# Packed attention and two MLPs on one core: the last 64 tokens of each sequence on all 128 partitions

## The chip, the cores and the metric

The kernel runs on one core of a Trainium2 chip. The metric is the device time of one launch in microseconds (us); the kernel before takes 1620.88 us in the median of three runs (1620.12 to 1622.61). The engines are PE (TensorE, matrix products; PEld is its loading of weights), DVE (VectorE), ACT (ScalarE), POOL (GpSimd) and SP (SyncE, which here only issues DMAs).

## What is computed

```python
def _attn_ref(q, k, v, p):              # q, k, v: 8 x 8 x 576 x 64; p: 8 x 8 x 32 x 64
    scale = 1.0 / np.sqrt(q.shape[-1])
    def sm_attn(qq, kk, vv):
        s = scale * np.matmul(qq, kk.transpose(0, 1, 3, 2))
        s = s - np.max(s, axis=-1, keepdims=True)
        a = np.exp(s)
        a = a / (np.sum(a, axis=-1, keepdims=True) + 1e-09)
        return np.matmul(a, vv)
    p_packed = sm_attn(p, k, v)
    return sm_attn(q, p_packed, p_packed)

x = attn_out.transpose(0, 2, 1, 3).reshape(4608, 512)
xn = x / rms(x) * rms_g                 # first MLP, d_ff 1536
x = (silu(xn @ w_gate) * (xn @ w_val)) @ w_out
h = x @ w_in2                           # second MLP, d_ff 2048
out = (h * sigmoid(1.702 * h)) @ w_out2
```

All inputs and the output are 32-bit floats.

## The kernel before

The 64 attention problems (8 batches of 8 heads) are worked in 16 chains: one chain is four heads of one batch. A chain loads its k, v and q (`load_kp`, `load_v`, `load_q`), transposes k and q on PE (`heads_t`, L297), multiplies p with k (`scores`, L308), takes the softmax (`s1`), transposes its weights (`a_t`, L341), multiplies them with v (`pv`, L353), transposes the result (`pp_t`, L374), multiplies it with q (`s2`), and forms the attention output (`x`, L443) for the row norm, whose reciprocal `ri` is spread over the partitions by five more transposes (`scale`, L474), once for each batch.

A sequence has 576 tokens: NC = 5 pieces, four of 128 and one of REST = 64. `GROUPS` puts pieces 0 and 1 into half e = 0 and pieces 2, 3 and 4 into half e = 1. The last piece lies in partitions 0 to 63 of its tile; `size(c)` is 64 for it and 128 otherwise, and cuts the partitions that an instruction reads. The letter a counts the two pairs of heads of a chain: a transpose takes two heads (2 x 64 columns) at a time. So a chain has ten transposes of k and ten of q, two of each on 64 rows.

The first four chains (LEAD, the lead below) run at the start in full 32-bit precision, with their own pool and loads of k in one piece (`kw`, then a copy on DVE into `kn`). The other twelve split each operand into a rounded high part and a low part (`split`: a copy on ACT, a subtraction on DVE or POOL; `split_v` for v), and three products stand for one. They are put between the matmuls of the first MLP (`mlp1`: `prods` L679, `gateval` L712, `project` L748), which is paced by a list of ns that each of its steps is taken to last. The second MLP (`mlp2`, L1068 and L1140) follows.

The order on each engine is set by a scheduler that works from the program order and its own estimate of times; only instructions marked `keep_in_program_order` stay where they are written, among them the loads of the chains after the lead. All loads are issued by SP, one after the other. Before each one but the first eight, SP waits for the landing of the load that stands eight before it. The tiles of the transposes, scores and products are PSUM banks: 3 of the 8 belong to attention (`ap`), 5 to the MLP (`mm`).

Of the kernel before, what the change touches and what calls it, by code (L numbers as in the profile page):

```python
# [32 lines left out]
def tile_pack_attention__then__two_mlps(  # L33
# [24 lines left out]
    P = 128  # L58
# [89 lines left out]
    def attention(at, first, lp, psum, getL, getAT):  # L148
# [37 lines left out]

        def load_kp(n):
# [5 lines left out]
            rest = k[b, h0 : h0 + HG, S - REST :].rearrange("h p d -> p h d")  # L193
            if n < WIDE:
                kw = at.tile([P, HG, NC - 1, D], F32, tag="kq", name="kw", bufs=nb)
                load(n, kw, k[b, h0 : h0 + HG, : S - REST].rearrange("h (p c) d -> p h c d", c=NC - 1))
                load(n, kn[:REST, NC - 1], rest)
                for a in range(2):
                    hs = slice(2 * a, 2 * a + 2)
                    nc.vector.tensor_copy(kn[:, : NC - 1, hs].rearrange("p c h d -> p h c d"), kw[:, hs])  # L200
            else:
                for h in range(HG):
                    load(n, 
                        kn[:, : NC - 1, h, :], k[b, h0 + h, : S - REST].rearrange("(p c) d -> p c d", c=NC - 1)
                    )
                load(n, kn[:REST, NC - 1], rest)
# [9 lines left out]
        def load_v(n):  # L216
# [6 lines left out]
            vs = vn[:, :head].rearrange("p (h c d) -> p h c d", h=HG, d=D), vn[:REST, head:]  # L223
# [7 lines left out]
        def load_q(n):  # L231
            b, g = chains[n]
            qn = at.tile([P, NC, HG, D], F32, tag="kq", name="qn", bufs=2)
            hs = slice(HG * g, HG * g + HG)
            rest = q[b, hs, S - REST :].rearrange("h p d -> p h d")
            for h in range(HG):
                load(n, 
                    qn[:, : NC - 1, h, :], q[b, HG * g + h, : S - REST].rearrange("(c p) d -> p c d", p=P)
                )
            load(n, qn[:REST, NC - 1], rest)  # L240
            st[n]["qn"] = qn

        def split_v(n):
# [6 lines left out]
            head = (NC - 1) * HG * D  # L250
            for part in ((slice(None), slice(head)), (slice(REST), slice(head, NC * HG * D))):
                i = nc.scalar.copy(vh[part], vn[part])
                if n == LEAD:
                    tc.keep_in_program_order(i)
                nc.gpsimd.tensor_sub(vl[part], vn[part], fl(vh[part]))
            st[n]["v"] = vh, vl

        def v_of(t, c):
# [4 lines left out]
            return t[:REST, head:].rearrange("p (h d) -> p h d", h=HG)  # L263
# [21 lines left out]
        def heads_t(n, name, a, e):  # L285
# [9 lines left out]
            for c in GROUPS[e]:  # L295
                o = c * P - cols.start
                nc.tensor.transpose(  # L297
                    ps[:, o : o + size(c)],
                    src[: size(c), c, 2 * a : 2 * a + 2, :].rearrange("p h d -> p (h d)"),
                    ident[: size(c), : size(c)],  # L300
                )
            split([t[:, a, cols] for t in st[n][name + "T"]], ps[:, : cols.stop - cols.start], nc.vector)
# [30 lines left out]
        def a_t(n, e):  # L333
# [6 lines left out]
            for i, c in enumerate(GROUPS[e]):  # L340
                nc.tensor.transpose(ps[: size(c), i], e1[:, c * P : c * P + size(c)], ident)  # L341
            c0, c1 = GROUPS[e][0], min(GROUPS[e][-1] + 1, NC - 1)
            split([t[:, c0:c1] for t in st[n]["aT"]], ps[:, : c1 - c0], nc.vector)
            if NC - 1 in GROUPS[e]:
                split([t[:REST, NC - 1] for t in st[n]["aT"]], ps[:REST, NC - 1 - c0], nc.vector)

        def pv(n):
# [115 lines left out]
        def scale(b, *es):  # L463
# [5 lines left out]
            for e in es:  # L469
                ps = psum()  # L470
                cols = span(e)
                for c in GROUPS[e]:
                    o = c * P - cols.start
                    nc.tensor.transpose(  # L474
                        ps[:, o : o + size(c)],
                        ri[: size(c), c : c + 1].to_broadcast([size(c), P]),
                        ident[: size(c), : size(c)],
# [896 lines left out]
```

## Time and profile before

| | before |
|---|---|
| median of three runs | 1620.88 us |
| the profiled execution's own time | 1620.02 us |
| its span in the trace | 1618.2 us |
| PE busy | 1593.0 us (98%) |
| DVE, ACT, POOL busy | 68%, 54%, 57% |
| chain that ended last | PE 90%; DMA, DVE, ACT, issue 2% each |
| granted PE clock | 0.998 |

The profile is of one execution; 1.8 us of that execution's own time lie outside of the span. Busy time of PE runs from a matmul's start to its modelled end, and matmuls overlap, so what one matmul costs is read from the distance of the starts of two that follow each other. `128*128 128x256` in a row of PE is the weights (rows*columns) and the moving operand.

### The profile page before, as it was taken

The numbers are of one execution on the slowest core, as the hardware profiler recorded it, in microseconds if no ns is written. First come the engines' busy times: TensorE is split into PE (matmuls) and PEld (weight loads), VectorE is DVE, ScalarE is ACT, GpSimd is POOL, SyncE is SP. The second block draws the span as 40 slices with busy tenths as digits, with TensorE's granted clock in tenths as the row PEclk, the third lists the DMA queues.
The fourth block names the chain that finished last, engine by engine and source line by source line (L and its number), as shares of the span: only waits on it lengthen the run. The fifth ranks groups of instructions, "written<-read, shape, count | busy, mean of one in ns | idle before, by whom it ended". The sixth has DMA issues, their size and how long they took to land.

```text
span 1618.2 us, 29102 instructions
## 1 busy us (share of the span) xinstructions
PE 1593.0 (98%) x10608; PEld 1510.4 (93%) x10608; DVE 1094.5 (68%) x1899; ACT 870.6 (54%) x1799; POOL 915.7 (57%) x749
## 2 busy tenths in 40 slices
PE   7999999999999999999999999999999999999998
PEld 5699999999999999999999899999999999999998
DVE  5777777767777766676775567754685467468466
ACT  5677777666566655665665353534344434435432
POOL 3547777656655566563655275664466445546442
PEclk9999999999999999999999999999999999999999
DMA  9766666775556665475454887786677667888874
GB/s 263 222 175 185 210 198 215 255 222 184 180 176 210 204 193 180 150 250 204 153 204 149 316 282 241 235 248 187 183 225 248 189 186 240 288 247 252 285 232 143
DMA packets 217725, 348.21 MB, mean 215 GB/s; under 512 B 93936, under 2 KB 123632, under 8 KB 211440
## 3 DMA queue, kind: packets, MB, share of 16 engines
q1 hardware_dynamic: 217584, 346.35, 66.9%
q8 instruction: 85, 1.39, 0.4%
q14 instruction: 56, 0.46, 0.1%
HBM read 279.19 MB, written 67.11 MB: 214 GB/s over the span
## 4 chain that ended last, share of the span: by engine, by line
PE 90%; DMA 2%; DVE 2%; ACT 2%; issue 2%; POOL 1%; SPq 0%; POOLq 0%; DVEq 0%; ACTq 0%
PE ps_dn L1140 21%; PE ps_up L1068 20%; PE ps_o L748 18%; PE ps_g L712 18%; PE ps_w L679 4%; PE ps_at L308 3%; PE ps_at L297 2%; PE ps_at L353 2%; PE ps_at L443 2%; DMA kw<-in_k_dram 1%; DMA vn<-in_v_dram 1%; POOL ol L1114 1%; PE ps_at L341 0%; DMA raw<-in_moe_w_out_dram 0%; DVE Wl L684 0%
## 5 line engine op out<-in xcount | busy, mean ns | idle before, releaser
L1114 POOL TENSOR_TENSOR ol<-g,oh 128x1024 fp32r<-128x1024 f32 (+1 forms) x117 | 258.9, 2223 | 295.7 <-ACT oh L1112 292.9
L1140 PE MATMUL ps_dn<-wo,oh 128*128 128x256 f32 x2016 | 366.2, 283 | 1.8 <-ACT oh L1112 0.9
L1140 PEld LDWEIGHTS ps_dn<-wo,oh 128*128 128x128 f32 x2016 | 318.6, 191 | 8.7 <-ACT oh L1112 1.3
L748 PE MATMUL ps_o<-Hh,wo 128*128 128x384 f32 x1152 | 320.3, 340 | 0.1
L1140 PE MATMUL ps_dn<-wo,ol 128*128 128x256 f32 x1008 | 279.6, 284 | 0.9 <-POOL ol L1114 0.9
L712 PE MATMUL ps_g<-Aqh,Wh 128*128 128x288 f32 x768 | 231.7, 302 | 4.0 <-DVE th L722 2.7
L712 PE MATMUL ps_g<-Aql,Wh 128*128 128x288 f32 x768 | 226.2, 295 | 0.0
L712 PE MATMUL ps_g<-Aqh,Wl 128*128 128x288 f32 x768 | 226.0, 295 | 0.0
L734 POOL TENSOR_TENSOR Hl<-th,Hh 128x576 fp32r<-128x576 f32 x96 | 138.4, 1442 | 138.3 <-ACT Hh L733 138.1
L1068 PE MATMUL ps_up<-x_t,wi 128*128 128x512 f32 (+1 forms) x936 | 213.6, 368 | 0.0
L748 PEld LDWEIGHTS ps_o<-Hh,wo 128*128 128x128 f32 x1152 | 209.9, 188 | 2.1 <-DVE th L725 0.3
L748 PE MATMUL ps_o<-Hl,wo 128*128 128x384 f32 x576 | 194.2, 337 | 0.0
L1140 PEld LDWEIGHTS ps_dn<-wo,ol 128*128 128x128 f32 x1008 | 190.7, 192 | 2.2 <-POOL ol L1114 1.5
L1091 ACT ACTIVATE g<-g 128x512 f32<-128x512 f32 (+1 forms) x120 | 70.7, 589 | 219.9 <-DVE g L1088 120.0
L684 DVE TENSOR_TENSOR Wl<-ps_w,Wh 64x512 fp32r<-64x512 f32 x192 | 131.8, 687 | 82.6 <-ACT Wh L683 79.8
L1068 PEld LDWEIGHTS ps_up<-x_t,wi 128*128 128x128 f32 x936 | 166.1, 188 | 18.7
L763 POOL TENSOR_TENSOR acc<-acc,add 128x384 f32<-128x384 f32 x135 | 139.0, 1041 | 50.1 <-ACT add L761 48.8
L1068 PE MATMUL ps_up<-x_b,wi 128*128 128x512 f32 (+1 forms) x702 | 164.4, 368 | 0.0
L1112 ACT CAST oh<-g 128x1024 fp32r<-128x1024 f32 (+1 forms) x120 | 113.4, 961 | 94.6 <-PE ps_dn L1140 63.4
L683 ACT CAST Wh<-ps_w 64x512 fp32r<-64x512 f32 x192 | 111.7, 582 | 81.7 <-PE ps_w L679 50.3
L712 PEld LDWEIGHTS ps_g<-Aqh,Wh 128*128 128x128 f32 x768 | 144.1, 188 | 8.2 <-DVE th L722 3.2
L1167 DVE TENSOR_TENSOR acc<-acc,ps_dn 128x512 f32<-128x512 f32 (+1 forms) x160 | 99.0, 630 | 71.9 <-PE ps_dn L1140 62.1
(203 smaller groups left out, 3258.3 us busy)
## 6 DMA issues: line engine op xcount, KB each, us to landing
wo<-wo SPq DMA_DIRECT2D x188, 512.0 KB, 4.0
wi<-wi SPq DMA_DIRECT2D x274, 256.0 KB, 3.8
wg<-wg SPq DMA_DIRECT2D x48, 1024.0 KB, 6.4
raw<-in_moe_w_out_dram SPq DMA_DIRECT2D x28, 512.0 KB, 4.4
wi<-stage SPq DMA_DIRECT2D x24, 512.0 KB, 4.1
wo<-stage SPq DMA_DIRECT2D x24, 512.0 KB, 3.7
x<-acc SPq DMA_DIRECT2D x32, 288.0 KB, 3.4
vn<-in_v_dram SPq DMA_DIRECT2D x16, 512.0 KB, 6.8
```

Of the source, the lines that this page charges most:

```text
L683: nc.scalar.copy(Wh[rows, :, g], src)
L684: nc.vector.tensor_sub(Wl[rows, :, g], src, fl(Wh[rows, :, g]))
L712: nc.tensor.matmul(ps, st[:, o, g, c * P : (c + 1) * P], mv[:, g, cols], start=n == 0, stop=n == 3 * NG - 1)
L734: nc.gpsimd.tensor_sub(Hl, th, fl(Hh))
L748: nc.tensor.matmul(ps, st[:, m * P : (m + 1) * P], mv[:, cols], start=n == 0, stop=n == 3 * len(ss) - 1)
L763: nc.gpsimd.tensor_add(a, a, t)
L1068: nc.tensor.matmul(o, w[:, y, k], x[:, z, k], start=i == 0 and not go_on, stop=i == 5, skip_group_check=bool(go_on))
L1091: nc.scalar.activation(gf, o if q == "a12" else gf, AF.Gelu_apprx_sigmoid)
L1112: nc.scalar.copy(oh, src)
L1114: (nc.vector if late else nc.gpsimd).tensor_sub(ol, src, fl(oh))
L1140: nc.tensor.matmul(o[:, r], x[:, a, (r0 + r) * P : (r0 + r + 1) * P], w[:, a, y], start=i == 0 and not go_on, stop=i == 6 * m - 1, skip_gr ...
L1167: nc.vector.tensor_add(z, z, o[:, :m])
```

## The change

The rest of k and of q is loaded by two DMAs instead of one (`last`): the first pair of heads into partitions 0 to 63, the second pair into partitions 64 to 127, side by side in the first 128 columns. One transpose of 128 rows then gives the last 64 columns of both pairs. It stands with the first pair (a = 0); its 128 columns leave PSUM in two pieces, the first pair's with the rest of half 1, the second pair's on its own.

The rest of v goes to partitions 64 to 127, and POOL sets partitions 0 to 63 to zero there. The softmax weights' last transpose takes columns 448 to 575 instead of 512 to 575, so that the last 64 tokens lie in partitions 64 to 127 and the 64 tokens before meet zeros; the product with v reads all 128 rows. Half 1 of these weights leaves PSUM in one piece instead of two, and v is split in one piece instead of two. The transposes of `ri` read all 128 rows.

```diff
+        def last(n, dst, src):
+            for a in range(2):
+                load(n, dst[a * REST : (a + 1) * REST, :2], src[2 * a : 2 * a + 2].rearrange("h p d -> p h d"))
...
-                load(n, kn[:REST, NC - 1], rest)
+                last(n, kn[:, NC - 1], rest)
...
-            vs = vn[:, :head].rearrange("p (h c d) -> p h c d", h=HG, d=D), vn[:REST, head:]
+            vs = vn[:, :head].rearrange("p (h c d) -> p h c d", h=HG, d=D), vn[P - REST :, head:]
+            nc.gpsimd.memset(vn[: P - REST, head:], 0.0)
...
-            load(n, qn[:REST, NC - 1], rest)
+            last(n, qn[:, NC - 1], rest)
...
-            for part in ((slice(None), slice(head)), (slice(REST), slice(head, NC * HG * D))):
-                i = nc.scalar.copy(vh[part], vn[part])
-                nc.gpsimd.tensor_sub(vl[part], vn[part], fl(vh[part]))
+            i = nc.scalar.copy(vh, vn)
+            nc.gpsimd.tensor_sub(vl, vn, fl(vh))
...
             for c in GROUPS[e]:
+                if c == NC - 1 and a:
+                    continue
                 nc.tensor.transpose(
-                    ps[:, o : o + size(c)],
-                    src[: size(c), c, 2 * a : 2 * a + 2, :].rearrange("p h d -> p (h d)"),
-                    ident[: size(c), : size(c)],
+                    ps[:, o : o + P], src[:, c, heads, :].rearrange("p h d -> p (h d)"), ident
                 )
-            split([t[:, a, cols] for t in st[n][name + "T"]], ps[:, : cols.stop - cols.start], nc.vector)
+            end = min(cols.stop, S - REST) if a else cols.stop
+            split([t[:, a, cols.start : end] for t in st[n][name + "T"]], ps[:, : end - cols.start], nc.vector)
+            if a == 0 and cols.stop == S:
+                o = S - cols.start
+                split([t[:, 1, S - REST :] for t in st[n][name + "T"]], ps[:, o : o + REST], nc.vector)
...
-                nc.tensor.transpose(ps[: size(c), i], e1[:, c * P : c * P + size(c)], ident)
+                c1 = c * P + size(c)
+                nc.tensor.transpose(ps[:, i], e1[:, c1 - P : c1], ident)
...
-                    x[: size(c), c],
+                    x[:, c],
...
-                        ri[: size(c), c : c + 1].to_broadcast([size(c), P]),
-                        ident[: size(c), : size(c)],
+                        ri[:, c : c + 1].to_broadcast([P, P]),
+                        ident,
```

On PE, where the first chain after the lead meets the first projection of the MLP (`qn` are the loaded queries, `ps_o` the projection's bank, `Wl` and `Hl` low parts), the order before is:

```order
L712 MATMUL ps_g<-Aqh,Wl 128x288
L297 MATMUL ps_at<-ident,qn 128x128 x2
L297 MATMUL ps_at<-ident,qn 128x64
L748 MATMUL ps_o<-Hh,wo 128x384
L748 MATMUL ps_o<-Hl,wo 128x384
L748 MATMUL ps_o<-Hh,wo 128x384 x2
```

and with the change:

```order
L721 MATMUL ps_g<-Aqh,Wl 128x288
L757 MATMUL ps_o<-Hh,wo 128x384
L757 MATMUL ps_o<-Hl,wo 128x384
L757 MATMUL ps_o<-Hh,wo 128x384 x2
L757 MATMUL ps_o<-Hl,wo 128x384
L757 MATMUL ps_o<-Hh,wo 128x384
L305 MATMUL ps_at<-ident,qn 128x128 x3
```

The 64-row transpose (written 128x64) has become the third of three full ones, and the group stands six projection matmuls later. In the whole program the 160 transposes each of k and q become 144 each, and no row with 64 rows is left among them.

On SP, the start of the loads (`kw` is k in one piece, `kn` its rest here, `pb` p) before:

```order
L183 DMA kw<-in_k_dram 128x4x256
L183 DMA kn<-in_k_dram 64x4x64
L183 DMA pb<-in_p_dram 64x4x64 x2
L183 DMA kw<-in_k_dram 128x4x256
L183 DMA kn<-in_k_dram 64x4x64
L183 DMA pb<-in_p_dram 64x4x64 x2
L183 DMA vn<-in_v_dram 128x4x256
```

and with the change:

```order
L183 DMA kw<-in_k_dram 128x4x256
L183 DMA kn<-in_k_dram 64x2x64 x2
L183 DMA pb<-in_p_dram 64x4x64 x2
L183 DMA kw<-in_k_dram 128x4x256
L183 DMA kn<-in_k_dram 64x2x64 x2
L183 DMA pb<-in_p_dram 64x4x64 x2
L183 DMA vn<-in_v_dram 128x4x256
```

The order is the same, with one load more for each k; the loads of q later grow in the same way, and those of v do not.

On POOL, where the second chain after the lead splits its v (`vl` is v's low part, `Hl` that of the MLP's hidden layer, `wg` of a weight), before:

```order
L255 TENSOR_TENSOR vl<-vn,vh 128x1024
L269 TENSOR_TENSOR pbm<-pb,mask_105 128x256
L255 TENSOR_TENSOR vl<-vn,vh 64x256
L141 TENSOR_TENSOR wg<-w,wg 128x4x128
L734 TENSOR_TENSOR Hl<-th,Hh 128x576 x2
```

and with the change:

```order
L260 TENSOR_TENSOR vl<-vn,vh 128x1280
L274 TENSOR_TENSOR pbm<-pb,mask_105 128x256
L141 TENSOR_TENSOR wg<-w,wg 128x4x128
L743 TENSOR_TENSOR Hl<-th,Hh 128x576
L230 MEMSET vn 64x256
L743 TENSOR_TENSOR Hl<-th,Hh 128x576
```

The two subtractions are one, and the zeros of the next chain's v stand behind the subtraction that is the last reader of the tile.

## Rows read from the trace of the kernel before

**Rows 1.** Windows: stretch, its length, busy us (instructions) by engine, clock, DMA share, GB/s.

```profile
20.00:40.00 20.00, 18.69 (x100) 13.72 (x100) 13.22 (x34) 13.61 (x41) 10.42 (x17) 1.00 1.07 284
60.00:80.00 20.00, 16.16 (x96) 12.48 (x94) 15.70 (x30) 14.14 (x39) 11.27 (x14) 1.00 0.55 168
80.00:720.00 640.00, 638.63 (x4387) 617.52 (x4387) 474.89 (x1008) 422.30 (x994) 414.63 (x426) 1.00 0.62 199
```

**Rows 2.** Waits of PE, 80 to 720 us, the longest: total us, times, longest.

```profile
PE ps_g L712 <- DVE Wl L684: 0.8, 1, 0.8
```

**Rows 3.** Timeline of PE: start, us, line, tiles, weights, moving operand; merged rows carry xcount.

```profile
91.89 0.58 PE L297 MATMUL ps_at<-ident,qn 128*128 128x128 f32 x3
...
92.00 0.27 PE L297 MATMUL ps_at<-ident,qn 128*128 128x128 f32 x1
...
92.20 0.27 PE L297 MATMUL ps_at<-ident,qn 64*128 64x64 f32 x1
...
92.40 0.44 PE L748 MATMUL ps_o<-Hh,wo 128*128 128x384 f32 x1
92.68 0.34 PE L748 MATMUL ps_o<-Hl,wo 128*128 128x384 f32 x1
...
93.75 0.38 PE L341 MATMUL ps_at<-ident,e 128*128 128x128 f32 x2
93.89 0.42 PE L748 MATMUL ps_o<-Hh,wo 128*128 128x384 f32 x1
94.14 0.49 PE L341 MATMUL ps_at<-ident,e 128*128 128x128 f32 x3
```

**Rows 4.** Timeline of PE, seven transposes of k, one of them on 64 rows.

```profile
81.10 1.17 PE L297 MATMUL ps_at<-ident,kn 128*128 128x128 f32 x7
82.02 0.51 PE L712 MATMUL ps_g<-Aqh,Wl 128*128 128x288 f32 x2
```

**Rows 5.** Timeline of PE, the end of a product with v.

```profile
100.00 0.28 PE L353 MATMUL ps_at<-vl,aTh 128*128 128x256 f32 x1
100.12 0.28 PE L353 MATMUL ps_at<-vh,aTl 128*128 128x256 f32 x1
100.33 0.39 PE L353 MATMUL ps_at<-vh,aTh 64*128 64x256 f32 x1
...
101.33 0.33 PE L748 MATMUL ps_o<-Hh,wo 128*128 128x384 f32 x1
```

**Rows 6.** Lines L297 and L474 after the lead: durations, first and last start, forms.

```profile
L297 PE MATMUL ps_at<-ident,qn x120: 270/272/276, 88.5 to 675.8; 128*128 128x128 f32 x96, 64*128 64x64 f32 x24
...
L474 PE MATMUL ps_at<-ident,ri x35: 266/272/275, 78.7 to 717.3; 128*128 128x128 f32 x28, 64*128 64x64 f32 x7
```

**Rows 7.** Chain of waits in the lead: start, us, what.

```profile
15.07 7.93 DMA kw<-in_k_dram
...
25.65 6.90 DMA kw<-in_k_dram
...
36.09 0.64 PE ps_at L297 x3
```

**Rows 8.** Timeline of SP's queue, issues of loads in the lead.

```profile
18.42 5.29 SPq L183 DMA_DIRECT2D qn<-in_q_dram  x5
...
26.30 0.60 SPq L183 DMA_DIRECT2D kn<-in_k_dram  x1
```

**Rows 9.** Groups by form: count, busy us, mean ns, idle time before.

```profile
L162 ACT CAST kTh<-ps_at 128x320 fp32r<-128x320 f32 x24 | 10.3, 427 | 3.2 <-PE ps_at L297 3.0
...
L162 ACT CAST kTh<-ps_at 128x256 fp32r<-128x256 f32 x24 | 9.0, 374 | 2.0 <-PE ps_at L297 1.8
...
L164 DVE TENSOR_TENSOR kTl<-ps_at,kTh 128x320 fp32r<-128x320 f32 x24 | 11.5, 480 | 0.3
...
L164 DVE TENSOR_TENSOR kTl<-ps_at,kTh 128x256 fp32r<-128x256 f32 x24 | 10.0, 415 | 1.4 <-ACT kTh L162 1.2
...
L255 POOL TENSOR_TENSOR vl<-vn,vh 64x256 fp32r<-64x256 f32 x12 | 9.0, 754 | 0.0
```

More of the change, by code (lines that the diff above doesn't have):

```diff
@@ L192, in load_kp @@
             kn = at.tile([P, NC, HG, D], F32, tag="kq", name="kn", bufs=nb)
-            rest = k[b, h0 : h0 + HG, S - REST :].rearrange("h p d -> p h d")
+            rest = k[b, h0 : h0 + HG, S - REST :]
             if n < WIDE:
@@ L205, in load_kp @@
                     )
-                load(n, kn[:REST, NC - 1], rest)
+                last(n, kn[:, NC - 1], rest)
             pb = at.tile([P, HG, D], F32, tag="pb", name="pb", bufs=bufs(n))
@@ L234, in load_q @@
             hs = slice(HG * g, HG * g + HG)
-            rest = q[b, hs, S - REST :].rearrange("h p d -> p h d")
+            rest = q[b, hs, S - REST :]
             for h in range(HG):
@@ L249, in split_v @@
             vh, vl = (at.tile([P, NC * HG * D], F32R, tag=f"v{x}", name=f"v{x}") for x in "hl")
-            head = (NC - 1) * HG * D
-            for part in ((slice(None), slice(head)), (slice(REST), slice(head, NC * HG * D))):
-                i = nc.scalar.copy(vh[part], vn[part])
-                if n == LEAD:
-                    tc.keep_in_program_order(i)
-                nc.gpsimd.tensor_sub(vl[part], vn[part], fl(vh[part]))
+            i = nc.scalar.copy(vh, vn)
+            if n == LEAD:
+                tc.keep_in_program_order(i)
+            nc.gpsimd.tensor_sub(vl, vn, fl(vh))
             st[n]["v"] = vh, vl
@@ L262, in v_of @@
                 return t[:, :head].rearrange("p (h c d) -> p h c d", h=HG, d=D)[:, :, c, :]
-            return t[:REST, head:].rearrange("p (h d) -> p h d", h=HG)
+            return t[:, head:].rearrange("p (h d) -> p h d", h=HG)
         def p_mask(n):
@@ L295, in heads_t @@
             for c in GROUPS[e]:
+                if c == NC - 1 and a:
+                    continue
                 o = c * P - cols.start
+                heads = slice(2 * a, 2 * a + 2)
                 nc.tensor.transpose(
[L298 to L302 removed]
+                    ps[:, o : o + P], src[:, c, heads, :].rearrange("p h d -> p (h d)"), ident
+                )
+            end = min(cols.stop, S - REST) if a else cols.stop
[3 more added lines that the diff above has]
+                split([t[:, 1, S - REST :] for t in st[n][name + "T"]], ps[:, o : o + REST], nc.vector)
         def scores(sts, mvs, e):
@@ L340, in a_t @@
             for i, c in enumerate(GROUPS[e]):
-                nc.tensor.transpose(ps[: size(c), i], e1[:, c * P : c * P + size(c)], ident)
-            c0, c1 = GROUPS[e][0], min(GROUPS[e][-1] + 1, NC - 1)
+                c1 = c * P + size(c)
+                nc.tensor.transpose(ps[:, i], e1[:, c1 - P : c1], ident)
+            c0, c1 = GROUPS[e][0], GROUPS[e][-1] + 1
             split([t[:, c0:c1] for t in st[n]["aT"]], ps[:, : c1 - c0], nc.vector)
-            if NC - 1 in GROUPS[e]:
-                split([t[:REST, NC - 1] for t in st[n]["aT"]], ps[:REST, NC - 1 - c0], nc.vector)
         def pv(n):
@@ L474, in scale @@
                     nc.tensor.transpose(
-                        ps[:, o : o + size(c)],
-                        ri[: size(c), c : c + 1].to_broadcast([size(c), P]),
-                        ident[: size(c), : size(c)],
+                        ps[:, o : o + P],
+                        ri[:, c : c + 1].to_broadcast([P, P]),
+                        ident,
                     )
```

## The prediction

> **What bounds the kernel now.** I read the page first: PE is busy for 98% of the span and stands in 90% of the chain that ended last. Then the windows, to find the stage that the change is in: from 80 to 720 us, where twelve of the sixteen chains run between the matmuls of the first MLP, PE is busy for 638.6 of 640 us, while DVE has 474.9 and ACT 422.3 [rows 1]. PE stands still there for 1.4 us, of which the longest wait, for the low part of a product of weights (`Wl`), takes 0.8 [rows 2]. So there the time is the sum of the distances between the starts of PE's instructions: what one of them takes less, the kernel takes less, as long as nothing else comes late. In the lead, 0 to 80 us, it is different: the chain of waits runs through two loads of k, issued at 15.07 and 25.65 us and landed 7.93 and 6.90 us later, and on PE from 36 us on [rows 7]; PE is idle for 1.3 us between 20 and 40, and from 60 to 80 us PE stands still for 3.8 us [rows 1].
>
> **What 64 rows cost on PE.** The timeline shows the price, and not in the row of the instruction itself (0.27 us, like a full transpose's) but in the starts [rows 3]. Two full transposes start 0.11 us apart (91.89, 92.00). The 64-row one starts 0.20 after the second, the next matmul 0.20 after it, and the matmul behind that 0.28 later. From the first transpose to the second projection matmul, 0.79 us pass. The comparison stands just below: two full transposes and a projection matmul take 0.39 us (93.75 to 94.14), so with a third full transpose it would be 0.50. The 64-row transpose thus costs 0.29 us more than a full one in its place, and 0.40 more than none: each change between 64 and 128 rows, in and out, costs PE some 0.1 us, and the instruction is not shorter itself. Where another transpose follows, it is less: the seven transposes at 81.10 take 0.92 us to the next matmul [rows 4]; seven full ones would take 6 x 0.11 and the 0.03 by which a matmul of another kind follows the last (0.14 from 93.75 to 93.89 less 0.11), 0.69. The difference is 0.23.
>
> The products with v pay likewise. From 100.12 to 101.33 us start four of them, of which the last three, from 100.33 on, have 64 rows, then two transposes and a projection matmul: 1.21 us [rows 5]. At the full-row distance of 0.12 (100.00 to 100.12) and the 0.39 of [rows 3] it would be 0.87, so the run costs 0.34; where a projection matmul follows at once, by the same count 0.39.
>
> The Trainium skill has a rule that says otherwise: "TensorE: Matmul & The Clock Gate", section on LDWEIGHTS, holds that a weight load takes as long for 32 rows as for 128, since only columns count, and by that alone an instruction with 64 rows would cost what a full one does and the change would save only the transposes that it drops. The instructions' own 0.27 us agree with it; the distances of the starts in [rows 3] do not, and they decide. The time that it would give is the second rival's below.
>
> **Part by part.** (1) *Transposes of k and q after the lead.* There are 48 on 64 rows, 24 of q [rows 6] and as many of k. By their starts in the timeline, 41 are followed by another kind of matmul and 7 by a transpose: 41 x 0.29 + 7 x 0.23 = 13.5 us if all were full. Half of them vanish instead: 24 x 0.11 = 2.6 more. Sum 16.1 us. (2) *Products with v after the lead.* Twelve chains, whose three 64-row products stand together six times and are parted by other matmuls six times: 18 pieces, each 0.34 to 0.39 [rows 5], at the middle 6.6 us. (3) *Transposes of ri.* Seven of the eight lie in this stretch [rows 6]: 7 x 0.29 = 2.0 us. (4) *The last transpose of the softmax weights* keeps its 128 moving columns; it gets more weight columns, not rows, and fewer columns cost nothing now: the three at 94.14, the last with 64, take 0.49 us, the two full ones at 93.75 take 0.38, and the 0.11 between them is a full one's distance [rows 3]. Nothing. **Together 24.7 us** of PE's time between 80 and 720 us.
>
> (5) *The lead* has 16 such transposes, four products with v and one transpose of ri: at the same prices 16 x 0.25 + 8 x 0.11 + 4 x 0.35 + 0.3 = 6.6 us, of which 3.8 lie behind 33 us, where PE is the chain (8 transposes, three products, ri). Against it stand the loads. Each k and each q takes one issue more on SP, which in the lead issues nearly without pause; ahead of the fourth chain's kw, at 25.65, come five more (three k, two q). At 0.60 us, an issue of kn, that is 3.0 us; at 5.29 / 5 = 1.06, one of q when SP waits for landings, 5.3 us [rows 8]. The other end is nothing: the bytes are the same, and the DMA engines' share is 1.07 in that stretch [rows 1], so that kw lands when its turn among the bytes comes. I take 3.0, since kn is what is added. PE behind 33 us then does 3.8 less but starts 3.0 later: the lead gains 0.8 us, in bounds of 6.6 gained (kw not later) and 1.5 lost (5.3 later). I take **1 us**. The zeros for the first v after the lead stand on POOL ahead of the last `Lh` of the lead and wait for a product on PE: at most half a us there, in these bounds.
>
> (6) *Work that other engines get.* Each k and q has one eviction more, 128x64. By the slope between 320 and 256 columns [rows 9] it takes 0.21 us on ACT and 0.22 on DVE, while the a = 1 eviction gets shorter by 0.05 and 0.07: 24 x 0.16 = 3.8 us on ACT and 24 x 0.15 = 3.6 on DVE. Merged evictions of the softmax weights and of v give back about as much on ACT and half of it on DVE. DVE then has some 477 us of work in about 615: 78% for 74%. The zeros cost POOL no more than the 0.75 us of a subtraction of the same shape, which goes as one of its own [rows 9]; that shape becomes part of a longer subtraction. All of this is hidden behind PE; if it were not, a us of it would cost a us. (7) *Order.* The scheduler has put the pieces of attention some matmuls earlier or later throughout. PE's idle time in this stretch is 1.4 us now [rows 1], and the same scheduler made that order. I take nothing, with 0 to 6 us for the range.
>
> **The sum** against the profiled execution's own 1620.0 us (its span is 1618.2): 1620.0 - 24.7 - 1.0 = 1594.3. That execution is 0.9 below the median of the three runs; against the median it is 1595.2. I forecast **1595 us**. The ends: with all of the lead's 6.6 and nothing lost, 1588.7; with 1.5 lost in the lead and 6 of new waits, 1602.8, or 1603.7 against the median.
>
> **The rivals.** *Given back on the way:* with PE 4% faster, DVE or ACT come last in the chains of attention, and PE waits for evictions as it now waits for `Wl`. For it: such a wait is there already [rows 2], and the splits are queued behind MLP work on the same engines. Against: all idle time is 1.4 us of 640, and DVE stays below 80%. If half of the 24.7 went so: 1620.9 - 12.4 - 1 = 1607.5. *Rows cost nothing:* only the 32 dropped transposes count, 32 x 0.11 = 3.5 us: 1617. For it speaks that a 64-row row is as long as a full one; against it the starts of [rows 3] and [rows 5]. *The bank is held too long (slower):* the bank of a = 0, e = 1 now empties by two evictions, and attention has three banks. If each of the 24 after the lead made PE wait for its next bank, the price is the second copy and subtraction, 0.21 + 0.22 us, and what stands ahead of them in the queues of ACT and DVE, two or three operations like the 0.37 to 0.48 us of [rows 9]: some 1.5 us, 24 x 1.5 = 36 less the 26 gained, 1631. It decides from 1.1 us a time. Against it: now, with 320 columns in such a bank, all waits of PE together are 1.4 us, and the longest is for something else [rows 1, 2]. *The change does not do what it says* would be 64-row instructions left over: the order shows none in transposes or products with v, so this has no chance worth a number.
>
> **How the numbers follow.** Forecast with its bounds (1588 to 1604) 0.83; half given back 0.08; rows cost nothing 0.03; the bank 0.03; other losses in the lead or by order that leave a gain of some 10 us 0.03. The range 1588 to 1604 holds the first and leaves the others out. About 0.2% (3 us) is what a measurement of this kernel can tell from no change. Faster by more than that: the first two, the lead's other losses and most of the second rival, 0.95; within it 0.02; slower 0.03.
>
> **What would show it.** In the profile after, the three transposes at the first projection should start 0.11 us apart with no 0.20 and no 0.28 behind them; the products with v all 0.12 apart; the first MLP's stretch should be shorter by some 25 us with as many us of waits as now, and its PE rows still above 99% busy. The fourth kw should be issued some 3 us later, and PE reach the end of the lead within 2 us of before. I am wrong if PE's waits in that stretch grow beyond 6 us, which the waits would show under evictions (`kT`, `qT`) or `Wl`; or if the starts keep their distances.

## The result, and the profile after

The changed kernel takes **1604.92 us** (median of 5 runs, 1603.70 to 1605.73) against 1620.12 us for the kernel before beside it (1619.39 to 1622.61): a ratio of 0.9901, with an interval of 0.9890 to 0.9913. It is faster, as forecast, but by 15 us and not by 26: the forecast was 1595 us with a range of 1588 to 1604, so the time lies 0.9 us above the range's end.

The profiled execution took 1603.8 us, 16.2 us less than the profiled one of before. Four marks in the two traces tell where they went, with the kernel before on the left. The lead ends (first `prods` matmul) at 62.15 and 63.26 us: 1.1 lost. From there to the first `project` matmul it is 30.25 and 29.88: 0.4 gained. From there to the first matmul of the second MLP it is 806.7 and 789.3: 17.4 gained. The second MLP takes 714.5 and 715.0. The first of the marks, before and after:

```profile
62.15 0.50 PE L679 MATMUL ps_w<-wg,Lh 128*128 128x256 f32 x2
```

```profile
63.26 0.48 PE L688 MATMUL ps_w<-wg,Lh 128*128 128x256 f32 x2
```

The windows of the kernel after, in the columns of [rows 1]:

```profile
20.00:40.00 20.00, 17.68 (x95) 14.27 (x94) 12.67 (x33) 12.22 (x40) 10.31 (x15) 0.92 1.04 289
60.00:80.00 20.00, 16.10 (x94) 12.74 (x93) 15.80 (x29) 14.37 (x41) 11.36 (x18) 1.00 0.62 183
80.00:720.00 640.00, 635.05 (x4485) 627.67 (x4484) 483.34 (x1041) 430.99 (x1015) 424.00 (x431) 1.00 0.64 207
```

PE works 98 more instructions into the same 640 us, and yet its idle time there has grown from 1.4 us [rows 1] to 4.95. From 20 to 40 us the granted clock is 0.92, where it was 1.00.

The timeline of PE shows the price of 64 rows gone (columns as in [rows 3]):

```profile
82.18 0.92 PE L305 MATMUL ps_at<-ident,kn 128*128 128x128 f32 x7
83.01 0.80 PE L721 MATMUL ps_g<-Aqh,Wl 128*128 128x288 f32 x4
...
94.20 0.49 PE L305 MATMUL ps_at<-ident,qn 128*128 128x128 f32 x3
94.53 0.38 PE L352 MATMUL ps_at<-ident,e 128*128 128x128 f32 x2
94.66 0.42 PE L757 MATMUL ps_o<-Hh,wo 128*128 128x384 f32 x1
...
101.41 0.28 PE L362 MATMUL ps_at<-vl,aTh 128*128 128x256 f32 x1
101.53 0.28 PE L362 MATMUL ps_at<-vh,aTl 128*128 128x256 f32 x1
101.65 0.38 PE L286 MATMUL ps_at<-ident,pbm 128*128 128x128 f32 x2
```

Three transposes of q now take 0.33 us from start to start of the next kind, 0.11 each, where [rows 3] had 0.20 before and 0.20 behind the 64-row one, and 0.28 behind the matmul that follows. The last products with v follow each other at 0.12, where [rows 5] needed 1.21 us for four of them and three more instructions. Seven transposes of k take 0.83 us for the 0.92 of [rows 4].

The waits of PE from 80 to 720 us, the longest (total us, times, longest), answer to [rows 2]:

```profile
PE ps_o L757 <- DVE acc L767: 0.8, 1, 0.8
PE ps_at L318 <- DVE kTl L164: 0.8, 2, 0.5
PE ps_at L305 <- DVE kTl L164: 0.7, 2, 0.4
PE ps_g L721 <- DVE Wl L693: 0.7, 1, 0.7
PE ps_o L757 <- DVE th L736: 0.5, 1, 0.5
```

One long wait of 0.8 us has become some ten of 0.2 to 0.8, and most come from DVE: `kTl` is the low part of the transposed k, `acc` the sum of the MLP, `th` its gate.

**How the losses are counted below.** PE's starts tell more than its waits, since the modelled end of a matmul covers a part of each wait. So for the stretch from the first `project` to the second MLP I took, for every pair of neighbouring PE instructions, the median distance of its kind (same shape, same kinds of neighbours, over all traces); their sum is PE's own time, and what the trace has beyond it is lost. Before, that is 799.2 own and 7.1 lost; after, 775.8 own and 13.1 lost. The two add up to 0.4 us less than the stretch in both kernels. Counted by shapes alone, it is 801.7 and 5.0 before, 778.2 and 11.1 after: other levels, but within 0.1 us the same differences. In the lead (from 6 us to its end, counted alike), before has 34.3 own and 21.8 lost; after has 27.5 and 29.6. Only the differences mean something there: the lead's products in full 32-bit precision start 0.22 us apart at 256 columns, the split ones behind it 0.12, and one price for both puts some 10 us of PE's own work in the lead under lost, in every kernel alike.

### The profile page after: what moved, and what is told of

Its sections match the earlier page's. It is cut to its first block, busy times and chain, and to the rows that moved or that the text cites. A ratio compares the mean times of both kernels' runs of the same rounds, so it can differ in the third digit from the quotient of the medians.

```text
span 1602.0 us, 29123 instructions
## 1 busy us (share of the span) xinstructions
PE 1566.8 (98%) x10576; PEld 1501.9 (94%) x10576; DVE 1089.9 (68%) x1911; ACT 867.6 (54%) x1803; POOL 918.8 (57%) x753
## 4 chain that ended last, share of the span: by engine, by line
PE 85%; DVE 4%; ACT 3%; DMA 3%; issue 2%; POOL 2%; SPq 1%; POOLq 0%; ACTq 0%; DVEq 0%
PE ps_dn L1149 21%; PE ps_up L1077 21%; PE ps_o L757 16%; PE ps_g L721 16%; PE ps_w L688 4%; PE ps_at L318 2%; PE ps_at L362 1%; PE ps_at L452 1%; DMA raw<-in_moe_w_out_dram 1%; PE ps_at L305 1%; SPq L183 1%; DMA vn<-in_v_dram 1%; ACT ps_at L461 0%; DVE w L131 0%; DVE Wl L693 0%
## 5 line engine op out<-in xcount | busy, mean ns | idle before, releaser
L1121 ACT CAST oh<-g 128x1024 fp32r<-128x1024 f32 (+1 forms) x120 | 113.4, 961 | 93.3 <-PE ps_dn L1149 63.3
```

Source lines behind the costliest of these rows:

```text
L1121: nc.scalar.copy(oh, src)
```

## Experiments

Medians are over 4 to 10 runs, and ratios are to the kernel before on the same chip, with intervals. Positions in a trace are those of one profiled execution each.

### The three parts apart

Each part of the change was made alone on the kernel before. The edit of the first is the hunks of `last`, `heads_t` and the loads of k and q:

```diff
-                load(n, kn[:REST, NC - 1], rest)
+                last(n, kn[:, NC - 1], rest)
...
+                if c == NC - 1 and a:
+                    continue
```

> The kernel before with the change of k and q alone (two loads for the rest, one 128-row transpose for both pairs); v, its product and ri stay on 64 rows. Theory A (the price of 64 rows on PE was right, and some 9 us of the gain were lost to waits: 2 in the lead by the later loads, 7 after it): PE's distances, idle time left out, lose 16 us after the lead, and the lead ends about 1 us later than before as in the changed kernel; the time is 16 to 12 us below before, so 1604 to 1608. Theory B (the price was too high): PE's distances of the transposes and what follows them lose 10 us or less; the time is 1609 to 1612.

Measured: 1611.29 us, ratio 0.9937 (0.9917 to 0.9956). PE's own time behind the lead is 784.5, so 14.7 less; 9.3 are lost, 2.2 more. The lead ends at 63.9 us, 1.7 later.

The second is the hunks of `load_v`, `split_v`, `v_of`, `a_t` and `pv`:

```diff
-            for part in ((slice(None), slice(head)), (slice(REST), slice(head, NC * HG * D))):
-                i = nc.scalar.copy(vh[part], vn[part])
...
+            i = nc.scalar.copy(vh, vn)
...
-                    x[: size(c), c],
+                    x[:, c],
```

> The changed kernel with k, q and ri as before: v's rest in the upper half with zeros below, product on 128 rows, v split and half 1 of the softmax weights evicted in one piece each. Theory A: PE's distances lose 6.6 us after the lead and 1.4 in it; if ACT's wait for v in one piece costs PE something, the time is 8 less 2 to 5, so 3 to 6 us below before: 1614 to 1617, with ACT waiting for v's loads 10 us or more in all (4.9 before). Theory B, and also a theory C that only the loads of k and q cost something: the full gain of what PE loses, 7 to 8 us, 1612 to 1613, with ACT's wait for v no longer than 6 us.

Measured: 1618.32 us, ratio 0.9982 (0.9972 to 0.9991). PE's own time is 792.4, 6.8 less, but 11.3 are lost, 4.2 more: most of what the full rows save is lost again. ACT waits 11.6 us for the loads of v. The lead ends at 62.0.

The third is the hunk of `scale`:

```diff
-                        ri[: size(c), c : c + 1].to_broadcast([size(c), P]),
-                        ident[: size(c), : size(c)],
+                        ri[:, c : c + 1].to_broadcast([P, P]),
+                        ident,
```

> The kernel before with the transposes of ri alone on 128 rows (8 in all). PE's distances lose 8 x 0.29 = 2.3 us. Theory A: 1618, and no new load or eviction, so what differs from that by more than 1 us is what another order by the scheduler does. Theory B: 1619 to 1620.

Measured: 1617.66 us, ratio 0.9977 (0.9967 to 0.9987). Own time 797.0, 2.2 less, 6.5 lost, and the lead ends at 61.5.

What follows: the three parts save 14.7, 6.8 and 2.2 us of PE's own time, 23.7 together, and the changed kernel 23.4. The additional losses behind the lead, 2.2, 4.2 and -0.6, add up to 5.8, and the changed kernel has 6.0. The prices of 64 rows and the losses belong to the parts, and the part with v gives most of its gain back.

### Where the part with v loses: one copy for two loads

In the kernel before, ACT copied the first 512 tokens of v as soon as the large load had landed, and the 64-row rest behind it. After, one copy needs both loads. ACT works in order, so everything behind the copy waits as well. ACT's waits for v from 80 to 720 us (total us, times, longest), first of the kernel before, then of the kernel after:

```profile
ACT vh L252 <- DMA vn<-in_v_dram: 4.9, 5, 2.0
```

```profile
ACT vh L257 <- DMA vn<-in_v_dram: 14.6, 7, 3.5
```

The chain of waits of the kernel after from 239 to 252 us (start, us, what) shows how one of them reaches PE:

```profile
239.11 5.94 DMA vn<-in_v_dram
...
245.13 0.29 ACT vh L257
...
246.30 0.61 ACT wg L140
246.91 0.57 ACT Hh L742
247.48 0.37 ACT add L770
247.86 0.55 ACT between L129
...
250.64 0.73 DVE kTl L164 x2
251.37 0.47 DVE acc L767
...
251.88 0.79 PE ps_o L757 x3
```

ACT idles for 3.5 us ahead of `vh`, then works off what has piled up behind it, `Hh` and a sum of the MLP among it; DVE waits for ACT, and PE for both: at 247.5, 249.5, 250.1 and 251.9 us its starts come 0.64, 0.44, 0.40 and 0.98 us late. The wait view has 0.39, 0.28, 0.16 and 0.82 for these.

The test gives each load its copy again, and with it its subtraction on POOL, and leaves all rows full:

```diff
-            i = nc.scalar.copy(vh, vn)
+            head = (NC - 1) * HG * D
+            for part in (slice(head), slice(head, NC * HG * D)):
+                i = nc.scalar.copy(vh[:, part], vn[:, part])
...
-            nc.gpsimd.tensor_sub(vl, vn, fl(vh))
+                nc.gpsimd.tensor_sub(vl[:, part], vn[:, part], fl(vh[:, part]))
```

> The changed kernel with the split of v in two copies and two subtractions again: one for the first 512 tokens, one for the block of the last 64 with its zeros. All PE instructions keep 128 rows. Theory (PE lost some 6 us between the first projection and the second MLP because ACT, in order, waits for both of v's loads at one copy): ACT's waits for the loads of v fall from 14.6 us to below 10, PE's losses in that stretch from 13 to about 9 us (the kernel before: 7), and the time is 2 to 4 us below the changed kernel's 1604.9: 1601 to 1603. Rival (the losses come from the order that the scheduler made, whatever v's copy waits for): losses stay at 12 to 14 us, time 1604 to 1606, up to 1 us slower for the extra operations.

Measured: 1601.98 us, ratio 0.9884 (0.9867 to 0.9900). Lost behind the lead: 9.6. ACT's waits for v in this kernel, from 80 to 720 us:

```profile
ACT vh L259 <- DMA vn<-in_v_dram: 7.6, 5, 1.8
```

In its timeline of ACT, the copies of the same v stand without a wait, and between them work that another engine needs:

```profile
247.70 1.06 ACT L259 CAST vh<-vn 128x1024 fp32r<-128x1024 f32 x1
248.65 0.23 ACT L162 CAST kTh<-ps_at 128x64 fp32r<-128x64 f32 x1
248.75 0.43 ACT L259 CAST vh<-vn 128x256 fp32r<-128x256 f32 x1
```

Of the wait views of PE between 110 and 260 us, that of the changed kernel has 2.8 us and this one 0.5. The merged operation thus cost some 3.5 us of the 6.0; the 9.6 that remain are about the 9.3 of the k and q part alone. The run splits the copy and the subtraction together; that it was the copy rests on the chain above, which goes through `vh` and not through POOL.

The last test on this issues v's loads two steps of the chain earlier, on top of the two copies and of the earlier fourth k (below):

```diff
-                do((heads_t, n, "q", 1, 0))
+                do((heads_t, n, "q", 1, 0), *([(load_v, m)] if m else []))
...
-                    do((load_v, m), (load_q, m), (p_t, m))
+                    do((load_q, m), (p_t, m))
```

> As the run before, and behind the lead the loads of a chain's v are issued two steps of the chain earlier (with the third group of q transposes of the chain before instead of behind its product with v). Theory (ACT's wait for v is the loss that is left over the kernel before): ACT's waits for v fall from 7.6 to below 4 us and PE's losses from 9.6 to 7 or 8, time 1 to 2 us below the run before. Rival (what is left comes from other splits and their order): ACT's waits fall, PE's losses stay at 9 to 10, time within 1 us.

Measured: 1600.41 us, ratio 0.9872 (0.9848 to 0.9895); the run before it took 1601.59, so within the scatter of both. Neither theory had its numbers: ACT's waits for v did not fall, they are 10.9 us, and PE's losses fell all the same, from 9.3 to 8.4 us. How long ACT waits in all is thus no measure of the harm. That it depends on what stands behind the waiting copy is a reading of the chain above, and no run shows it by itself.

### The lead

Forecast was a gain of 1 us in the lead; it lost 1.1. In the kernel after, the chain of waits there is:

```profile
13.09 4.08 DMA raw<-in_moe_w_gate_dram
17.26 0.62 ACT between L129
17.88 0.46 ACT kTh L162 x2
18.34 0.28 ACT aTh L162
18.67 3.70 PE ps_at L362 x10
```

Three more issues stand ahead of the first weights on SP, whose issue moves from 11.89 to 13.09 us: the two of k take 0.6 us each, while the six loads of q take SP 3.9 us where five took 4.0. ACT has the first step on them (L129) ahead of the copy of the softmax weights (`aTh`), waits 3.0 us, and PE waits for ACT:

```profile
PE ps_at L362 <- ACT aTh L162: 3.9, 1, 3.9
```

It was 0.6 us before. Nine kernels speak to the question what sets the end of the lead. The first takes the added issues away: one load for the last block of each k and q, with as many bytes, but of the last 128 tokens of the first pair of heads, so that it leaves out the second pair's and its output is not the attention's.

```diff
-            for a in range(2):
-                load(n, dst[a * REST : (a + 1) * REST, :2], src[2 * a : 2 * a + 2].rearrange("h p d -> p h d"))
+            load(n, dst[:, :2], src)
...
-            rest = k[b, h0 : h0 + HG, S - REST :]
+            rest = k[b, h0 : h0 + 2, S - P :].rearrange("h p d -> p h d")
```

> The changed kernel with one load instead of two for the rest of k and of q: it takes the last 128 tokens of the first pair of heads, so as many bytes and packets, but the scores of the last 64 tokens are of the wrong heads; all else is as in the changed kernel. Theory A: the first raw weights are issued near 11.9 us as before (13.1 in the changed kernel), PE's wait of 3.9 us for aTh near 15 us shrinks to under 2, the lead ends 2 us earlier, and the time is 2 to 4 us below the changed kernel: 1601 to 1603. If the lead's loss is the scheduler's order alone: the wait stays and the time is 1604 to 1606.

Measured: 1604.32 us, ratio 0.9889 (0.9867 to 0.9911). The fourth `kw` is issued at 25.1 us, as before the change, and the wait of 3.9 us is 0.9; but the lead ends at 63.6 us, and 2.9 us of PE's waits now stand behind a step of the softmax (`nm`). The added issues are not the whole of it, or something takes their place.

The second fetches the first weights ahead of the first q (and the small vector of the norm behind them):

```diff
+                while todo[0][0] < -29.5:
+                    act(todo.pop(0)[1])
+                for _ in range(2):
+                    fetch()
```

> The changed kernel with the first two fetches of w_gate and w_val issued on SP ahead of the first chain's six loads of q, the third fetch behind them, and the small g vector last. Theory A (the lead loses because the three added issues put the first weights 1.2 us later, ACT waits for them in order ahead of the copy of the first softmax weights, and PE for that): PE's 3.9 us wait ahead of the first product with v falls below 1.5, the clock stays at 1.0 from 20 to 40 us, and the first project of w_out (end of the lead) moves from 63.3 to 62 us or less; time 1603 to 1604. Theory B (the end of the lead hangs on the fourth chain's scores, which stand behind products with v): the wait goes, but the end of the lead stays within 0.5 us of 63.3, time 1604 to 1606.

Measured: 1605.85 us, ratio 0.9912 (0.9897 to 0.9926). The wait for `aTh` is gone, as theory A had it, and a wait for the third chain's k has come in its place (total, times, longest, 6 to 64 us):

```profile
PE ps_at L305 <- DVE kn L206: 5.4, 1, 5.4
...
PE ps_at L362 <- ACT aTh L162: 0.8, 1, 0.8
```

The third and the fourth `kw` are issued 1.8 and 1.2 us later than in the changed kernel, the clock from 20 to 40 us is 0.83, and the lead ends at 64.2. So theory A falls: this wait was not what the end of the lead hung on.

The third is for theory B, the order. In the kernel before, four groups of `scores` stood one after the other on PE at 38.5 us; in the changed kernel the scheduler put part of a product with v and of an `x` ahead of the fourth chain's second group, and its exponential starts at 47.2 instead of 44.5 us. One due time puts the scores together again:

```diff
-                do(t0 + 4.2, (s1, n, 1))
+                do(t0 + (3.9 if n == LEAD - 1 else 4.2), (s1, n, 1))
```

> The changed kernel with one number of the lead's table changed: the second half of the fourth chain's scores has its due time 0.3 earlier, so that the code writes it ahead of the third chain's product with v and the first chain's product with the weights, and PE's order there is that of the kernel before again (four groups of scores in a row). Theory B (this order delays the fourth chain's softmax, and with it the end of the lead): its exp starts at 45 to 46 us (now 47.2, before 44.5), the end of the lead comes at 61.3 to 62.3 us for 63.3, time 1603 to 1604 against 1604.9. Theory A (late weights alone): the end of the lead stays at 63 to 63.5, time 1604.5 to 1605.5.

Measured: 1604.67 us, ratio 0.9902 (0.9887 to 0.9917). The exponential starts at 46.9 us, and the lead ends at 64.3: theory B falls as well. PE's order was as wanted, but ACT's had changed with it, and squares of `x` stood ahead of the exponentials.

With this and the two copies and the early weights together:

```diff
+            for part in (slice(head), slice(head, NC * HG * D)):
...
+                for _ in range(2):
+                    fetch()
...
+                do(t0 + (3.9 if n == LEAD - 1 else 4.2), (s1, n, 1))
```

> The changed kernel with all three edits: v split in two copies, the first weights fetched ahead of the first q, and the fourth chain's scores ahead of the product with v. If the three losses are separate and each theory holds: the end of the lead at 60 to 61.5 us, PE's losses between the first projection and the second MLP at 9 us, time 1598 to 1601. If order alone makes the losses, whatever the edit: 1603 to 1607.

Measured: 1600.75 us, ratio 0.9880 (0.9866 to 0.9895): lost behind the lead 8.4 us, the lead ends at 63.5. The time is within the forecast for separate losses, the lead is not: it stays where it was.

Next, the fourth chain's k, since up to here the lead had ended 27 to 32 us after the copies of that k began in every kernel:

```diff
-                do(t0 - 50 if n < 2 else t0 - 2 * period + 2.6, (load_kp, n))
+                do(t0 - 50 if n < 2 else period * (n - 2) + 2.6 if n < LEAD - 1 else 3.4, (load_kp, n))
```

> The changed kernel with one due time of the lead's table changed: the loads of the fourth chain's k and p (five issues) stand on SP ahead of the second chain's q loads instead of behind them; PE's order in the lead stays what it is but for two pairs of transposes. Theory (in every kernel so far the lead ends 27 to 30 us after the fourth chain's k has landed, whatever PE has to do, so the lead's loss comes from that load's later issue): the fourth kw is issued at 20 to 23 us instead of 27.5, its copies to kn start at 28 to 31 us instead of 33.9, and the lead ends 2 to 4 us earlier, at 59 to 61 us; time 1601 to 1603 against 1604.9. Rival (vector work, in its order, bounds the lead, and the load only happens to stand with it): kn earlier, the lead still ends at 62.5 to 64.5 us, time 1604 to 1606.

Measured: 1604.77 us, ratio 0.9899 (0.9871 to 0.9927). The copies of that k start at 26.2 us, 7.7 earlier, and the lead ends at 64.0. This theory falls clearly: that load only stood beside the end of the lead. On SP, other loads have moved back for it; ACT now waits 2.4 us for weights at 34.6 us. With the two copies on top:

```diff
+            for part in (slice(head), slice(head, NC * HG * D)):
...
+                do(t0 - 50 if n < 2 else period * (n - 2) + 2.6 if n < LEAD - 1 else 3.4, (load_kp, n))
```

> Both the split of v in two copies and the earlier loads of the fourth chain's k. If the loss in the lead and the loss behind it are separate: the lead ends at 59 to 62 us, PE's losses from the first projection to the second MLP are 9 to 10 us, time 1598 to 1600. If the earlier load does nothing: 1601 to 1603.

Measured: 1601.59 us, ratio 0.9876 (0.9852 to 0.9899), lost behind the lead 9.3, end of the lead 64.6: what two copies give alone.

Two tests then part the issues from PE's work. One adds the issues to the kernel before and changes nothing else; its PE instructions keep 64 rows:

```diff
-                load(n, kn[:REST, NC - 1], rest)
+                last(n, kn[:REST, NC - 1], rest)
...
+                load(n, dst[:, 2 * a : 2 * a + 2], src[:, 2 * a : 2 * a + 2])
```

> The kernel before, with one edit: the load of the last 64 tokens of each k and q is issued as two loads of two heads each, as the changed kernel issues it (the same bytes to the same places, one more issue on SP for each). PE's instructions and their order in the lead stay those of before. If the added issues alone move the lead: the fourth kw is issued at 27 to 28 us (before 25.6), the lead ends 1 to 2 us later than 62.2, and the time is 1 to 2 us above the kernel before. If PE's work sets the end of the lead, or the order does: it ends within 0.4 us of 62.2, time the same within 1 us.

Measured: 1623.23 us, beside 1621.02 of the kernel before; ratio 1.0007 (0.9997 to 1.0018), so the time doesn't show a loss. In the profiled execution the first weights are issued at 12.87 us, the fourth `kw` at 27.50, and the lead ends 2.0 us later. Of these 1.2 are made up again by the end of the execution, 1.0 of them in the second MLP, whose time scatters by more than that. From its chain of waits, where the same steps stand as in the changed kernel, and from its timeline:

```profile
12.87 4.18 DMA raw<-in_moe_w_gate_dram
17.14 0.62 ACT between L129
18.44 4.26 PE ps_at L357 x10
```

```profile
64.13 0.50 PE L683 MATMUL ps_w<-wg,Lh 128*128 128x256 f32 x2
```

The other has the changed kernel's PE work, but neither the added issues (its one load leaves out the second pair of heads, as above) nor the scores behind the product with v:

```diff
+            load(n, dst[:, :2], src)
...
+                do(t0 + (3.9 if n == LEAD - 1 else 4.2), (s1, n, 1))
```

> The changed kernel with one load for the last block of each k and q (128 rows of two heads: the same number of bytes but other rows, so its outputs differ from the reference's) and with the fourth chain's scores due 0.3 earlier. It takes away both the added issues and the order in which scores stand behind the product with v. If issues and order each bound the lead and have to go together: exp of the fourth chain at 44.5 to 45.5 us, the lead ends at 61 to 62 us, time 2 us below the changed kernel: 1602 to 1603. If the vector engines, in order, bound it whatever comes first: it ends at 63 to 64 us, 1604 to 1605.

Measured: 1603.46 us, ratio 0.9887 (0.9865 to 0.9909). Its PE has 6.7 us less of its own to do in the lead than the kernel before, with as many issues and the scores in the same place, and the lead does not end earlier:

```profile
62.83 0.48 PE L687 MATMUL ps_w<-wg,Lh 128*128 128x256 f32 x2
```

The exponential of the fourth chain, at 45.8 us, is still 1.3 later than before: the order on ACT and DVE is not that of the kernel before.

The last joins what helped behind the lead, and takes the small loads off SP:

```diff
+                if n < LEAD:
+                    nc.gpsimd.dma_start(to, part)
+                else:
+                    load(n, to, part)
```

> The changed kernel with v split in two copies, v loaded two steps sooner behind the lead, the fourth chain's scores due 0.3 earlier, and in the lead the two loads of the last 64 tokens issued on POOL's DMA queue (POOL is busy 1.8 of the first 20 us) instead of SP's. If the issues on SP bound the lead: the first weights are issued at about 10.5 us (13.1 in the changed kernel), the fourth kw at 22 to 24, the lead ends at 60.5 to 62 us; with PE's losses behind it at 8 to 9 us the time is 1597 to 1599. If not: the lead ends at 63 to 64 us, time 1600 to 1602.

Measured: 1599.06 us (1595.85 to 1599.48), ratio 0.9852 (0.9825 to 0.9879), the fastest of all, 6 to 8 us below the changed kernel (by the medians, and by the ratios). PE's losses behind the lead are 7.8 us, nearly the 7.1 of the kernel before. The lead again ends at 64.2: its fourth `kw` is issued at 24.6 us, but its copy starts at 33.8 us, as in the changed kernel (33.9).

The lead in one table (us; PE's own and lost time from 6 us to its end):

| kernel | fourth kw issued | its copy starts | lead ends | PE own | lost |
|---|---|---|---|---|---|
| before | 25.6 | 32.6 | 62.2 | 34.3 | 21.8 |
| issues added to it (e12) | 27.5 | 34.3 | 64.1 | 34.3 | 23.8 |
| after | 27.5 | 33.9 | 63.3 | 27.5 | 29.6 |
| after, one load (e4) | 25.1 | 31.8 | 63.6 | 27.7 | 29.8 |
| one load, scores together (e13) | 25.2 | 32.3 | 62.8 | 27.6 | 29.2 |
| fourth k early (e9) | 20.2 | 26.2 | 64.0 | 27.6 | 30.4 |
| small loads on POOL's queue (e14) | 24.6 | 33.8 | 64.2 | 27.7 | 30.3 |

What follows: in the lead the change took 6.8 us off PE's own time, as worked out, and all of it was lost again, in waits and in part at a lower clock (last section). No kernel with the full rows of k and q ended its lead earlier than the kernel before. The added issues can cost up to 2.0 us there (e12, one execution). What exactly bounds the lead stays open: the loads from 20 to 50 us, with a DMA share at or above 0.94 in each ten us of it in the kernel after and in e9 (1.04 or more in the kernel before), ACT and DVE in the scheduler's order, and PE's clock are left, and no run here parts them.

## Why the prediction was wrong, point by point

The traces differ by 16.2 us where 25.7 were forecast. The 9.5 us between them are: 6.0 more lost behind the first `project`, 2.1 in the lead, 0.9 between these two, and 0.5 in the second MLP, which took 713.5 to 715.9 us in all sixteen kernels and is scatter.

**(1) to (3), the price of 64 rows: right.** Forecast 16.1, 6.6 and 2.0 us for 80 to 720 us; measured from the first `project` on, at 92.40 us, 14.7, 6.8 and 2.2. Three of the 55 transposes on 64 rows stand ahead of that mark, and so do some that are dropped or moved behind it. Counted by shapes alone and from the end of the lead, where the eighth transpose of `ri` is in it too, PE's own time falls by 25.0 us: 23.5 behind the first `project` and 1.5 ahead of it. Of these 1.5 only 0.4 came out as time. So the account above, with 23.4 and 0.4, stands 0.9 below the forecast 24.7, and this 0.9 is a wait and no price. The lower price, 0.23 where another transpose follows, holds as well. Here are five transposes of k with a 64-row one as the third (a merged row shows the form of its first), and then five full ones of the changed kernel:

```profile
250.47 0.95 PE L297 MATMUL ps_at<-ident,kn 128*128 128x128 f32 x5
251.18 0.42 PE L748 MATMUL ps_o<-Hh,wo 128*128 128x384 f32 x1
```

```profile
325.05 0.71 PE L305 MATMUL ps_at<-ident,kn 128*128 128x128 f32 x5
325.52 0.42 PE L757 MATMUL ps_o<-Hh,wo 128*128 128x384 f32 x1
```

They take 0.71 and 0.47 us to the next matmul, 0.24 apart. The one run of seven shows less, 0.92 [rows 4] and 0.83 after, since its last step to the next matmul is 0.17 there and not the 0.03 of [rows 3]; why, no run shows. The Trainium skill, in "TensorEngine Tiling (Array Packing)", Tiling Modes, Key Properties, says that changing the tiling mode drains the engine. It gives no time; the traces agree in that each change between 64 and 128 rows costs, and give some 0.1 us for it [rows 3]. That rows cost nothing, the second rival, is out: it would have saved 3.5 us.

**(4), the softmax weights' last transpose:** nothing, as forecast; the parts' sum leaves no room for more.

**(6), hidden work: the step that failed.** It priced merged evictions by their length and called them a gain. It did not ask what the merged copy of v waits for. Both loads had to be there now, ACT's waits for v went from 4.9 to 14.6 us, and the MLP's work stood behind it in the queue; two copies won 3.5 us back (e5). The further 2.2 come with k and q (e1); which of its steps does it was not tried.

**(7), order: nothing was taken, 0 to 6 for the range.** The extra losses are 6.0, the end of that range. The argument for nothing, 1.4 us of idle time before, says only that the old pieces fitted; it says nothing about new ones. PE's idle time from 80 to 720 us grew from 1.4 to 4.95 us, below the 6 us that were named as the limit, but the starts show the full 6.

**(5), the lead: wrong in sign.** PE's saving was right (6.8 for 6.6), the later issue of the fourth `kw` was 1.9 for the 3.0 taken. The failed step is that 3.8 us of the saving behind 33 us would count because the chain of waits ran on PE there [rows 7]. A chain that runs on PE shows that PE had work at every moment, not that others would be ready sooner had PE less. The first added issues, ahead of the first weights, were not looked at either: ACT's in-order wait for them cost 3.3 us more at the first product with v, though the end of the lead did not hang on it (e6).

**The sum.** Its two unfavourable ends, 1.5 lost in the lead and 6 of new waits, were given as the end of the range; both came nearly true at once (1.1 and 6.0), and the 0.9 and 0.5 put the time past it. The first rival, half given back by evictions that come late, had a part of the mechanism, PE waiting for DVE and ACT, and foresaw about twice the measured size: 6.0 of 23.8 is a quarter, and 3.5 of the 6.0 came by the copy of v and its load. The bank that is held too long did not show: PE's waits for `kTl` are 1.5 us in all.

## What to carry to other kernels

Price a change of rows in the distances of the starts around it, up to the second instruction behind it: here the forecast of PE's own time held within 4%. Then ask of every merged operation which of its inputs lands last, and what stands behind it on an engine that works in order: here the merged copy of v saved ACT 0.22 us at a time (1.27 for 1.06 and 0.43), twelve times, and the merging cost 3.5 us of PE's time. Where PE is the chain but stands among loads and evictions, as in a lead, make the forecast once with PE's saving at zero; it was zero here.

## What was not expected of the hardware

PE's clock fell in the lead. In the changed kernel the 3.9 us wait at 14.8 us is followed by a granted clock of 0.85 from 20 to 30 us, where the kernel before has 1.00:

```profile
20.00:30.00 10.00, 9.42 (x48) 7.62 (x47) 4.51 (x15) 5.94 (x21) 4.50 (x8) 0.85 1.01 253
```

The ten records of the product with v behind the wait take 3.70 us; the ten at 54.46 us take 2.32. The last ones there start 0.43 us apart and not 0.22: that is the lower of the clock's two levels, 1.2 GHz for 2.4. In the kernel before with two loads (e12), with a shorter wait of 1.7 us there, the ten take 4.26 us at a clock of 0.89 from 20 to 30 us.

The waits alone don't tell when the clock falls. With the part of v alone (e2) it is 0.83 from 10 to 20 us, although PE's longest wait from 8 to 20 us is 1.6 us, as in the kernel before; with the part of `ri` alone (e3) it stays at 1.00 behind waits of 1.6 and 1.3 us. Every kernel with the full rows of k and q has such a stretch in its lead (0.83 from 30 to 40 us in e13, 0.77 from 20 to 30 in e14), so a part of what the table calls lost there is a slower clock and not waiting. Whether it moves the end of the lead is open: in e2 the lead ended at 62.0 us all the same.
